# Retention by two chunks at a time: scores in a row, values in a row, K^T V at places of its own

## The chip, the cores and the metric

The kernel runs on one core of a Trainium2 chip. The metric is the device time of one execution in microseconds. "Ratio" is the mean time of one kernel's fast runs over that of the kernel before in the same rounds, so it is not quite the ratio of the medians that stand beside it. "Faster" or "slower" is said of a difference above 2%; smaller ones are called "same", though their intervals may exclude 1.

## The reference

Two stages in fp32: retention (linear attention with a decay by head) and a maxout FFN on its output.

```python
# q, k, v: (8, 8, 576, 64); gamma by head
scores = scale * np.matmul(q, k.transpose(0, 1, 3, 2))
ret = scores * Dmat                      # gamma**(i-j) where i >= j, else 0
attn = np.matmul(ret, v)
x = attn.transpose(0, 2, 1, 3).reshape(4608, 512)
h = np.maximum(np.maximum(x @ w1, x @ w2), x @ w3)     # 512 -> 768
out = h @ w_out                                        # 768 -> 512
```

## The kernel before

The 4608 tokens are cut into 36 chunks of 128 for the retention and into 9 tiles of 512 for the FFN. A sequence of 576 tokens doesn't end with a chunk, so some chunks hold the end of one sequence and the start of the next (`start_of`). Within a chunk, the kernel computes masked scores times values; what lies further back comes from a running state, K^T V summed over chunks.

```python
def load(g, *between):              # 16 small DMAs each for q and kx, then k and v
    for n, src in () if g < BY_PE else (("q", q), ("kx", k)):      # BY_PE: chunks 0-6 go another way
        t = raws[n, g] = raw.tile(..., bufs=3 if n == "q" else 2)
        for blk in range(C // 32):
            for a in range(4):
                nc.sync.dma_start(...)                             # 16 KB each
    ...                                                            # k and v, on nc.sync too
def decay_values(g):                # GpSimd: vd = v * gk
def transposes(g):                  # VectorE: kT from kx, qT from q (g >= BY_PE)
def scores(g):
    for p in range(NP):
        for j in range(2):
            r = slice(D * j, D * (j + 1))                          # 64 rows: two row tiles
            nc.tensor.matmul(s[j][:, p, :], lhsT=kT[r, p, :], rhs=qT[r, p, :], start=True, stop=True)
    ...                                                            # VectorE: mask into st
    r = start_of(g) or 0
    for p in range(NP):                                            # K^T V, in the same visit
        nc.tensor.matmul(kv[:, p, :], lhsT=pair(kr, p)[r:], rhs=pair(vds[g], p)[r:], start=True, stop=True)
    t = states[g + 1] = stp.tile([P, NP, P], FP32, tag="state", name="state")
    ...
        nc.vector.tensor_tensor(t[:], kv[:], states[g][:], op=ALU.add)
        nc.gpsimd.tensor_tensor(t[:], t[:], gs[:], op=ALU.mult)
def values(g):
    ...   # vd x st into o: 64 columns, two column tiles; then state x qT; VectorE: o * gq into xT
```

FFN tile t and the retention of the next four chunks are interleaved by hand. The FFN of a tile is a generator of 12 steps: nine units of up products (Strassen-like, seven products each, from tile 1 on) and three of the down products. Its output stores are issued by SyncE, like all loads; tile 0 also converts the weights from 64-bit floats.

```python
for t in range(N // NT):
    work = ffn(t)
    for g in range((t + 1) * CPT, (t + 2) * CPT):
        for step in (transposes, scores, values):
            if g < NG:
                if step is transposes and g + 1 < NG:
                    load(g + 1)
                if step is scores and g + 1 < NG:
                    decay_values(g + 1)
                if g > CPT or step is not transposes:
                    step(g)
            next(work, None)
```

Of the kernel before, what the change touches and what calls it, by code (L numbers as in the profile page):

```python
# [34 lines left out]
FP32 = mybir.dt.float32  # L35
# [4 lines left out]
ALU = mybir.AluOpType  # L40
PSUM = bass.MemoryType.PSUM

C = 128
NT = 4 * C
# [7 lines left out]
def kernel(  # L52
# [14 lines left out]
    nc = tc.nc  # L67
    P = 128
    B, H, S, D = q.shape
    N, DM = out.shape  # L70
    DF = moe_w1.shape[1]
    NP = H // 2
    NG = B * S // C
    NDC = DM // P
    NF = DF // P
    CPT = NT // C
# [3 lines left out]
    raw = ctx.enter_context(tc.tile_pool(name="raw", bufs=AHEAD + 1))  # L80
    vpool = ctx.enter_context(tc.tile_pool(name="vpool", bufs=3))
    att = ctx.enter_context(tc.tile_pool(name="att", bufs=2))
    stp = ctx.enter_context(tc.tile_pool(name="stp", bufs=2))
    xpool = ctx.enter_context(tc.tile_pool(name="xpool", bufs=2))
    spool = ctx.enter_context(tc.tile_pool(name="spool", bufs=1))
    hpool = ctx.enter_context(tc.tile_pool(name="hpool", bufs=1))
# [5 lines left out]
    ps_r = ctx.enter_context(tc.tile_pool(name="ps_r", bufs=4, space=PSUM))  # L92
# [5 lines left out]
    gq = const.tile([P, NP, C], FP32, name="gq")  # L98
# [17 lines left out]
    def start_of(g):  # L116
        r = -g * C % S
        return r if r < C else None
# [8 lines left out]
    raws, vds, qks, sts, states = {}, {}, {}, {}, {}  # L127

    def spans(g):

        row = 0
        while row < C:
            b, pos = divmod(g * C + row, S)
            n = min(C - row, S - pos)
            yield row, b, pos, n
            row += n

    def load(g, *between):
        rows = (("k", k), ("q", q), ("v", v)) if g < BY_PE else (("k", k), ("v", v))
        for n, src in () if g < BY_PE else (("q", q), ("kx", k)):  # L140

            t = raws[n, g] = raw.tile([P, NP, C // 32, 32], FP32, tag=n, name=n + "raw", bufs=3 if n == "q" else 2)
            for blk in range(C // 32):
                b, pos = divmod(g * C + 32 * blk, S)
                for a in range(4):
                    nc.sync.dma_start(
                        t[32 * a:32 * a + 32, :, blk, :],
                        src[b, a // 2::2, pos:pos + 32, 32 * (a % 2):32 * (a % 2) + 32].rearrange("p j i -> j p i"))
        for n, src in rows:
            if n == "v":  # L150
                for t, what in between:
                    nc.sync.dma_start(t[:], what)
            t = raws[n, g] = raw.tile([C, H, D], FP32, tag=n, name=n + "raw", bufs=4 if n == "k" else 3)
            for row, b, pos, m in spans(g):
                nc.sync.dma_start(t[row:row + m], src[b, :, pos:pos + m, :].rearrange("h p d -> p h d"))  # L155

    def decay_values(g):
        t = vds[g] = vpool.tile([C, H, D], FP32, tag="vd", name="vd")
        nc.gpsimd.tensor_tensor(t[:], raws.pop(("v", g))[:], gk[:].unsqueeze(2).to_broadcast([C, H, D]),  # L159
                                op=ALU.mult)  # L160

    def pair(t, p):
        return t[:, 2 * p:2 * p + 2, :].rearrange("a h d -> a (h d)")

    def transposes(g):
        both = qks[g] = {}
        if g >= BY_PE:
            for n in ("k", "q"):
                t = both[n] = att.tile([P, NP, C], FP32, tag=n + "T", name=n + "T", bufs=2 if n == "k" else 3)
                nc.vector.transpose(t[:].rearrange("a p c -> a (p c)"),  # L170
                                    raws.pop(("kx" if n == "k" else n, g))[:].rearrange("a p b i -> a (p b i)"))
            return
        for n, src in (("k", raws["k", g]), ("q", raws.pop(("q", g)))):
            pt = ps_r.tile([P, NP, C], FP32, tag="r", name=n + "t")
            for p in range(NP):
                nc.tensor.transpose(pt[:, p, :], pair(src, p), ident[:C, :C])
            t = both[n] = att.tile([P, NP, C], FP32, tag=n + "T", name=n + "T", bufs=2 if n == "k" else 3)
            nc.scalar.copy(t[:], pt[:])

    def scores(g):  # L180
        qT, kT = qks[g]["q"], qks[g]["k"]
        s = [ps_r.tile([C, NP, C], FP32, tag="r", name=f"s{j}") for j in range(2)]
        for p in range(NP):
            for j in range(2):
                r = slice(D * j, D * (j + 1))
                nc.tensor.matmul(s[j][:, p, :], lhsT=kT[r, p, :], rhs=qT[r, p, :], start=True, stop=True)  # L186
        st = sts[g] = att.tile([C, 2, NP, C], FP32, tag="st", name="st", bufs=2)
        for j in range(2):
            nc.vector.tensor_tensor(st[:, j], s[j][:], masks[start_of(g)][:].unsqueeze(1).to_broadcast([C, NP, C]),  # L189
                                    op=ALU.mult)  # L190
        kr = raws.pop(("k", g))
        if g + 1 == NG or start_of(g + 1) == 0:
            return
        r = start_of(g) or 0
        kv = ps_r.tile([P, NP, P], FP32, tag="r", name="kv")
# [3 lines that stand above are left out]
        if start_of(g) is not None:  # L199
            nc.vector.tensor_tensor(t[:], kv[:], gs[:], op=ALU.mult)  # L200
        else:
            nc.vector.tensor_tensor(t[:], kv[:], states[g][:], op=ALU.add)
            nc.gpsimd.tensor_tensor(t[:], t[:], gs[:], op=ALU.mult)

    xT, xS = {}, {}

    def values(g):
        old = C if start_of(g) is None else start_of(g)
        t, i = divmod(g, CPT)
        if i == 0:  # L210
            xT[t] = xpool.tile([P, NDC, NT], FP32, tag="xT", name="xT")
        st, vr, qT = sts.pop(g), vds.pop(g), qks.pop(g)["q"]
        o = ps_r.tile([P, NP, C], FP32, tag="r", name="o")
        for p in range(NP):
            for j in range(2):
                nc.tensor.matmul(o[D * j:D * (j + 1), p, :], lhsT=vr[:, 2 * p + j, :], rhs=st[:, j, p, :],  # L216
                                 start=(p == 0), stop=(old == 0 and p == NP - 1), skip_group_check=True)
        if old > 0:
            sd = states.pop(g)
            for p in range(NP):  # L220
                nc.tensor.matmul(o[:, p, :old], lhsT=sd[:, p, :], rhs=qT[:, p, :old],  # L221
                                 start=False, stop=(p == NP - 1), skip_group_check=True)
        nc.vector.tensor_tensor(xT[t][:, :, i * C:(i + 1) * C], o[:], gq[:], op=ALU.mult)  # L223
        if i == CPT - 1 and t > 0:
            x = xT[t]
            a11, a12, a21, a22 = (x[:, 2 * d:2 * d + 2, NH * r:NH * (r + 1)] for r in range(2) for d in range(2))
            s1, s2, s3, s4 = (spool.tile([P, 2, NH], FP32, tag=f"S{n}", name=f"S{n}") for n in (1, 2, 3, 4))
            nc.vector.tensor_tensor(s1[:], a21, a22, op=ALU.add)
            nc.vector.tensor_tensor(s2[:], s1[:], a11, op=ALU.subtract)
            nc.gpsimd.tensor_tensor(s3[:], a11, a21, op=ALU.subtract)  # L230
            nc.gpsimd.tensor_tensor(s4[:], a12, s2[:], op=ALU.subtract)
            xS[t] = {1: a11, 2: a12, 3: s4[:], 4: a22, 5: s1[:], 6: s2[:], 7: s3[:]}
# [200 lines left out]
    def convert(n):  # L433
        for _ in range(n):
            next(converting, None)
# [119 lines left out]
    warm(2)  # L555
    decay_values(1)
    scores(0)
    transposes(1)
    values(0)
    decay_values(2)  # L560
    scores(1)
    transposes(2)
    values(1)
    decay_values(3)
    scores(2)
    transposes(3)
    convert(2)
    values(2)
    convert(2)
    scores(3)  # L570
    decay_values(4)
    convert(2)
    values(3)
    transposes(4)
    convert(4)
    for t in range(N // NT):
        work = ffn(t)
        for g in range((t + 1) * CPT, (t + 2) * CPT):
            for step in (transposes, scores, values):
                if g < NG:  # L580
                    if step is transposes and g + 1 < NG:
                        load(g + 1)
                    if step is scores and g + 1 < NG:
                        decay_values(g + 1)
                    if g > CPT or step is not transposes:
                        step(g)
                next(work, None)


# [49 lines left out]
```

## Time and profile before

| | before |
|---|---|
| median (3 runs) | 830.7 us (830.61 to 830.96) |
| span of the profiled run | 828.2 us |
| TensorE, VectorE busy | 99%, 52% of the span |
| start of tile 1's first product | 130.18 us |
| tiles 1 to 7 (to the start of tile 8) | 622.30 us |
| tile 8 (no retention beside it) | 75.7 us |

The page in 40 equal slices (each digit is the tenths busy, or of full clock), and the head of its chain of work that ended last:

```profile
PE   9999999999999999999999999999999999999998
DVE  3999986455455544544454445444544435533342
PEclk9999999999999999999999999999999999999999
...
PE 86%; DVE 6%; issue 2%; SPq 2%; DMA 2%; ACT 1%; POOL 0%; DVEq 0%
```

TensorE (PE) is full from end to end at full clock, and it makes 86% of the chain. What the time can lose is TensorE work; what it can gain is any wait of TensorE.

### The profile page before, as it was taken

How to read it: one execution, taken by the hardware profiler on the slowest of the kernel's cores; microseconds unless marked ns; L12 is line 12 of the kernel's file. 1: busy time of each engine (PE TensorE's matmuls, PEld its weight loads, DVE VectorE, ACT ScalarE, POOL GpSimd, SP SyncE). 2: the span in 40 equal slices, each digit the busy share in tenths (PEclk: the TensorE clock that was granted, in tenths of full speed). 3: DMA queues.
4: the chain of work that ended last, by engine and by line, in shares of the span. 5: the costliest groups of instructions: out<-in, count | busy, mean ns of one | idle time of the engine just before them, and what ended most of it. 6: DMA issues, size and time to landing. Idle time of an engine off the chain costs nothing.

```text
span 828.2 us, 12659 instructions
## 1 busy us (share of the span) xinstructions
PE 821.8 (99%) x4616; PEld 668.8 (81%) x4616; DVE 434.5 (52%) x805; ACT 173.9 (21%) x401; POOL 192.3 (23%) x182
## 2 busy tenths in 40 slices
PE   9999999999999999999999999999999999999998
PEld 8555547888888888888888888888888888888887
DVE  3999986455455544544454445444544435533342
ACT  3766611111111111110111111111111011111211
POOL 3644665212111120113012111111111202201000
PEclk9999999999999999999999999999999999999999
DMA  9965431343133323332233223332333233201001
GB/s 231 302 169 155 104 70 45 57 79 63 51 55 57 56 79 57 57 57 56 58 73 61 60 52 57 56 58 79 57 57 55 59 75 58 46 13 39 1 1 51
DMA packets 236094, 59.33 MB, mean 72 GB/s; under 512 B 217088, under 2 KB 234496, under 8 KB 236032
## 3 DMA queue, kind: packets, MB, share of 16 engines
q1 hardware_dynamic: 235888, 58.53, 31.6%
q8 instruction: 36, 0.59, 0.3%
q14 instruction: 26, 0.21, 0.1%
q10 hardware_dynamic: 144, 0.00, 0.0%
HBM read 49.03 MB, written 9.44 MB: 71 GB/s over the span
## 4 chain that ended last, share of the span: by engine, by line
PE 86%; DVE 6%; issue 2%; SPq 2%; DMA 2%; ACT 1%; POOL 0%; DVEq 0%
PE x L446 30%; PE z L446 15%; PE dx L319 10%; PE y L446 8%; PE dz L319 5%; PE s L186 4%; PE o L216 4%; PE o L221 3%; PE kv L197 3%; PE dy L319 3%; PE down L495 2%; DVE expo L398 1%; SPq L155 1%; DVE frac L387 1%; DVE mant L393 1%
## 5 line engine op out<-in xcount | busy, mean ns | idle before, releaser
L446 PE MATMUL x<-S,T 128*128 128x256 f32 x576 | 147.9, 379 | 0.0
L159 POOL TENSOR_TENSOR vd<-vraw,gk 128x512 f32<-128x512 f32 x36 | 37.9, 1052 | 361.0 <-DMA vraw<-in_v_dram 342.2
L446 PEld LDWEIGHTS x<-S,T 128*128 128x128 f32 x576 | 109.0, 190 | 15.5 <-ACT u L451 0.3
L446 PE MATMUL x<-xT,w 128*128 128x256 f32 x288 | 74.8, 382 | 0.0
L476 DVE TENSOR_TENSOR tmp<-x,p 128x256 f32<-128x256 f32 x48 | 20.4, 425 | 103.5 <-PE x L446 103.5
L446 PE MATMUL x<-S,w 128*128 128x256 f32 x288 | 74.3, 380 | 0.0
L446 PE MATMUL z<-S,w 128*128 128x256 f32 x288 | 73.9, 379 | 0.0
L446 PE MATMUL y<-xT,w 128*128 128x256 f32 x288 | 73.9, 379 | 0.0
L446 PE MATMUL z<-xT,T 128*128 128x256 f32 x288 | 73.9, 379 | 0.0
L451 ACT COPY p<-x 128x256 f32<-128x256 f32 x72 | 26.8, 372 | 220.2 <-PE x L446 220.2
L189 DVE TENSOR_TENSOR st<-s,causal 128x512 f32<-128x512 f32 x72 | 46.3, 685 | 41.4 <-PE s L186 41.4
L504 PE MATMUL up<-xT,w 128*128 128x512 f32 x144 | 63.5, 594 | 0.2 <-POOL w L404 0.2
L446 PEld LDWEIGHTS z<-S,w 128*128 128x128 f32 x288 | 54.7, 190 | 7.4
L446 PEld LDWEIGHTS y<-xT,w 128*128 128x128 f32 x288 | 54.7, 190 | 7.4
L446 PEld LDWEIGHTS z<-xT,T 128*128 128x128 f32 x288 | 54.5, 189 | 7.7
L446 PEld LDWEIGHTS x<-S,w 128*128 128x128 f32 x288 | 49.3, 189 | 13.3 <-issue 1.3
L223 DVE TENSOR_TENSOR xT<-o,gq 128x512 f32<-128x512 f32 x36 | 24.9, 691 | 66.0 <-PE o L221 59.9
L446 PEld LDWEIGHTS x<-xT,w 128*128 128x128 f32 x288 | 51.5, 190 | 6.6 <-issue 0.8
L297 POOL TENSOR_TENSOR H<-h 128x256 f32<-128x256 f32 x24 | 17.9, 748 | 150.5 <-DVE h L489 150.5
L504 PEld LDWEIGHTS up<-xT,w 128*128 128x128 f32 x144 | 26.7, 190 | 30.7 <-issue 29.9
L465 DVE TENSOR_TENSOR tmp<-y,p 128x256 f32<-128x256 f32 x48 | 20.4, 425 | 52.7 <-PE y L446 52.7
L451 ACT COPY u<-x 128x256 f32<-128x256 f32 x72 | 26.8, 372 | 100.2 <-PE x L446 97.2
(92 smaller groups left out, 1233.6 us busy)
## 6 DMA issues: line engine op xcount, KB each, us to landing
bits<-in_moe_w_dram SPq DMA_DIRECT2D x18, 512.0 KB, 5.0
out_dram<-osb SPq DMA_DIRECT2D x35, 256.0 KB, 2.1
kraw<-in_k_dram SPq DMA_DIRECT2D x32, 256.0 KB, 3.0
vraw<-in_v_dram SPq DMA_DIRECT2D x32, 256.0 KB, 3.4
qraw<-in_q_dram SPq DMA_DIRECT2D x464, 16.0 KB, 1.8
kxraw<-in_k_dram SPq DMA_DIRECT2D x464, 16.0 KB, 1.8
bits<-in_moe_w_out_dram SPq DMA_DIRECT2D x6, 512.0 KB, 4.0
qraw<-in_q_dram SPq DMA_DIRECT2D x6, 256.0 KB, 5.1
```

The source lines that it names most:

```text
L159: nc.gpsimd.tensor_tensor(t[:], raws.pop(("v", g))[:], gk[:].unsqueeze(2).to_broadcast([C, H, D]), op=ALU.mult)
L186: nc.tensor.matmul(s[j][:, p, :], lhsT=kT[r, p, :], rhs=qT[r, p, :], start=True, stop=True)
L189: nc.vector.tensor_tensor(st[:, j], s[j][:], masks[start_of(g)][:].unsqueeze(1).to_broadcast([C, NP, C]), op=ALU.mult)
L197: nc.tensor.matmul(kv[:, p, :], lhsT=pair(kr, p)[r:], rhs=pair(vds[g], p)[r:], start=True, stop=True)
L216: nc.tensor.matmul(o[D * j:D * (j + 1), p, :], lhsT=vr[:, 2 * p + j, :], rhs=st[:, j, p, :], start=(p == 0), stop=(old == 0 and p == NP - ...
L221: nc.tensor.matmul(o[:, p, :old], lhsT=sd[:, p, :], rhs=qT[:, p, :old], start=False, stop=(p == NP - 1), skip_group_check=True)
L223: nc.vector.tensor_tensor(xT[t][:, :, i * C:(i + 1) * C], o[:], gq[:], op=ALU.mult)
L319: nc.tensor.matmul(out[m], lhsT=hS[n](fp)[:, m * P:(m + 1) * P], rhs=late["T"][n][:, fp, :], start=first and fp == 0 and (m == 0 or last a ...
L446: nc.tensor.matmul(out[:], lhsT=w[:, d * P:(d + 1) * P], rhs=xS[t][n][:, d, :], start=first and d == 0, stop=d == 1, skip_group_check=True)
L451: nc.scalar.copy(c[:], src[:])
L465: nc.vector.tensor_tensor(c11, y[:], p1[:], op=ALU.add)
L504: nc.tensor.matmul(ps[:], lhsT=w_sb[i, fb][:, dc * P:(dc + 1) * P], rhs=xT[t][:, dc, :], start=(dc == 0), stop=(dc == NDC - 1))
```

## The change

The intent is fewer changes of TensorE's tiling mode. The scores use TensorE as two tiles of 64 rows, the values as two tiles of 64 columns; a stretch of matmuls in one of the two modes is called a visit here. Two chunks a and b go together: both scores in one visit, both values in one visit, K^T V of each at another step. That needs a third state buffer, and in a tile's first pair b's scores three steps earlier than before (its transposes two). The core of the diff (the splitting of `scores` into `scores` and `state`, and the start-up part, are left out):

```diff
-    stp = ctx.enter_context(tc.tile_pool(name="stp", bufs=2))
+    stp = ctx.enter_context(tc.tile_pool(name="stp", bufs=3))
...
-    def values(g):
+    def values(*chunks):
...   # for all chunks: vd x st; then for all chunks: state x qT, and o * gq
+    def steps(g):
+        todo = [[] for _ in range(3 * CPT)]
+        for n in range(0, CPT, 2):
+            a, b, at = g + n, g + n + 1, 5 * (n // 2)
+            for c, k in ((a, at), (b, at + (g > CPT))):
+                if c + 1 < NG:
+                    todo[k].append(partial(load, c + 1))
+                if c > CPT:
+                    todo[k].append(partial(transposes, c))
+                if c + 1 < NG:
+                    todo[k].append(partial(decay_values, c + 1))
+            todo[at + 1] += [partial(scores, a), partial(scores, b)]
+            todo[at + 2].append(partial(state, a))
+            todo[at + 3].append(partial(state, b))
+            todo[at + 4].append(partial(values, a, b))
+        return todo
+
     for t in range(N // NT):
         work = ffn(t)
-        for g in range((t + 1) * CPT, (t + 2) * CPT):
-            for step in (transposes, scores, values):
...
+        for todo in steps((t + 1) * CPT) if t + 1 < N // NT else [[]] * 3 * CPT:
+            for step in todo:
+                step()
+            next(work, None)
```

More of the change, by code (lines that the diff above doesn't have):

```diff
@@ L190, in scores, with state @@
                                     op=ALU.mult)
+    def state(g):
         kr = raws.pop(("k", g))
@@ L205, with before @@
     xT, xS = {}, {}
-    def values(g):
-        old = C if start_of(g) is None else start_of(g)
-        t, i = divmod(g, CPT)
-        if i == 0:
-            xT[t] = xpool.tile([P, NDC, NT], FP32, tag="xT", name="xT")
-        st, vr, qT = sts.pop(g), vds.pop(g), qks.pop(g)["q"]
-        o = ps_r.tile([P, NP, C], FP32, tag="r", name="o")
-        for p in range(NP):
-            for j in range(2):
-                nc.tensor.matmul(o[D * j:D * (j + 1), p, :], lhsT=vr[:, 2 * p + j, :], rhs=st[:, j, p, :],
-                                 start=(p == 0), stop=(old == 0 and p == NP - 1), skip_group_check=True)
-        if old > 0:
-            sd = states.pop(g)
-            for p in range(NP):
-                nc.tensor.matmul(o[:, p, :old], lhsT=sd[:, p, :], rhs=qT[:, p, :old],
-                                 start=False, stop=(p == NP - 1), skip_group_check=True)
-        nc.vector.tensor_tensor(xT[t][:, :, i * C:(i + 1) * C], o[:], gq[:], op=ALU.mult)
+    def values(*chunks):
+        def before(g):
+            return C if start_of(g) is None else start_of(g)
+        o = {g: ps_r.tile([P, NP, C], FP32, tag="r", name="o") for g in chunks}
+        for g in chunks:
+            st, vr = sts.pop(g), vds.pop(g)
+            for p in range(NP):
+                for j in range(2):
+                    nc.tensor.matmul(o[g][D * j:D * (j + 1), p, :], lhsT=vr[:, 2 * p + j, :], rhs=st[:, j, p, :],
+                                     start=(p == 0), stop=(before(g) == 0 and p == NP - 1), skip_group_check=True)
+        for g in chunks:
+            t, i = divmod(g, CPT)
+            qT, old = qks.pop(g)["q"], before(g)
+            if old > 0:
+                sd = states.pop(g)
+                for p in range(NP):
+                    nc.tensor.matmul(o[g][:, p, :old], lhsT=sd[:, p, :], rhs=qT[:, p, :old],
+                                     start=False, stop=(p == NP - 1), skip_group_check=True)
+            if i == 0:
+                xT[t] = xpool.tile([P, NDC, NT], FP32, tag="xT", name="xT")
+            nc.vector.tensor_tensor(xT[t][:, :, i * C:(i + 1) * C], o[g][:], gq[:], op=ALU.mult)
         if i == CPT - 1 and t > 0:
@@ L557 @@
     scores(0)
+    state(0)
     transposes(1)
@@ L561 @@
     scores(1)
+    state(1)
     transposes(2)
@@ L565 @@
     scores(2)
+    state(2)
     transposes(3)
@@ L570 @@
     scores(3)
+    state(3)
     decay_values(4)
@@ L575 @@
     convert(4)
+    def steps(g):
[14 more added lines that the diff above has]
+        return todo
     for t in range(N // NT):
         work = ffn(t)
-        for g in range((t + 1) * CPT, (t + 2) * CPT):
-            for step in (transposes, scores, values):
-                if g < NG:
-                    if step is transposes and g + 1 < NG:
-                        load(g + 1)
-                    if step is scores and g + 1 < NG:
-                        decay_values(g + 1)
-                    if g > CPT or step is not transposes:
-                        step(g)
-                next(work, None)
+        for todo in steps((t + 1) * CPT) if t + 1 < N // NT else [[]] * 3 * CPT:
+            for step in todo:
+                step()
+            next(work, None)
 _INS = ['q', 'k', 'v', 'moe_w1', 'moe_w2', 'moe_w3', 'moe_w_out']
```

## The prediction

> **What bounds the kernel now.** I read the page's busy table first, then the windows by stage, then the merged timeline of one steady stage on TensorE, SyncE, VectorE and GpSimd, and last the waits. Tile t of the FFN (512 tokens) runs while the retention of the next four chunks is worked in between; a tile has 12 steps, nine "units" (7 Strassen products each) and three of the down projection.
>
> ```profile
> PE 821.8 (99%) x4616; PEld 668.8 (81%) x4616; DVE 434.5 (52%) x805; ACT 173.9 (21%) x401; POOL 192.3 (23%) x182
> ...
> 27.70:130.00 102.30, 101.59 (x401) 51.93 (x401) 97.45 (x142) 52.79 (x81) 63.18 (x47) 1.00 0.52 144
> 218.20:308.00 89.80, 89.80 (x530) 76.91 (x529) 43.35 (x83) 13.75 (x38) 15.84 (x15) 1.00 0.30 60
> ```
>
> The window lines give length, then PE, PEld, DVE, ACT, POOL busy, clock, DMA share and GB/s. From tile 1 on TensorE is the bound without a gap, at full clock; in tile 0 (27.7 to 130) VectorE is nearly as full (97.5 of 102.3), since it converts the weights. So a saving must be TensorE time, and any stall of TensorE is paid in full.
>
> Where TensorE loses time inside the retention shows in the start times (start, length, line, what):
>
> ```profile
> 222.48 1.03 PE L446 MATMUL z<-xT,T 128*128 128x256 f32 x4
> 223.34 1.08 PE L446 MATMUL x<-S,w 128*128 128x256 f32 x4
> 224.35 1.16 PE L186 MATMUL s<-qT,kT 64*128 64x128 f32 x16
> 225.44 1.16 PE L197 MATMUL kv<-vd,kraw 128*128 128x128 f32 x8
> 226.44 1.03 PE L446 MATMUL x<-xT,w 128*128 128x256 f32 x4
> ...
> 231.62 1.03 PE L446 MATMUL x<-S,w 128*128 128x256 f32 x4
> 232.58 1.09 PE L216 MATMUL o<-st,vd 128*64 128x128 f32 x16
> 233.60 1.16 PE L221 MATMUL o<-qT,state 128*128 128x128 f32 x8
> 234.59 1.03 PE L446 MATMUL x<-xT,w 128*128 128x256 f32 x4
> ```
>
> An ordinary product takes 0.86 us from start to start (222.48 to 223.34); the one before the scores takes 1.01. The scores use 64 rows (two row tiles), the values 64 columns (two column tiles), all else the full array.
>
> The second thing that matters is how the data of the next chunk come in:
>
> ```profile
> 218.16 1.03 PE L446 MATMUL x<-xT,w 128*128 128x256 f32 x4
> 218.36 0.65 ACT L369 COPY osb<-dx 128x256 f32<-128x256 f32 x2 [9.24 <-PE dx L319]
> 219.46 7.61 SPq L146 DMA_DIRECT2D qraw<-in_q_dram  x16
> 227.10 8.49 SPq L146 DMA_DIRECT2D kxraw<-in_k_dram  x16
> 235.69 1.28 SPq L155 DMA_DIRECT2D kraw<-in_k_dram  x2
> 237.07 1.27 SPq L155 DMA_DIRECT2D vraw<-in_v_dram  x2
> ...
> 242.44 0.70 DVE L170 STREAM_TRANSPOSE kT<-kxraw 128x512 f32<-128x512 f32 x1
> 243.06 0.66 DVE L170 STREAM_TRANSPOSE qT<-qraw 128x512 f32<-128x512 f32 x1
> 246.78 1.16 PE L186 MATMUL s<-qT,kT 64*128 64x128 f32 x16
> ```
>
> A load of one chunk keeps SyncE busy for 17 to 19 us: 32 small DMAs of q and k at 0.47 us of issue each, plus k and v. This load (chunk b, the tile's second) starts at 219.46, only after the last output store of the tile before, which waits for ScalarE's copy at 218.36. Its last transposable k lands at 236.85, its v at 240.77 (landing times in the trace). Before, VectorE wants it at 242.44, a little later, so nobody pays. The waits confirm that SyncE's queue stops at stores and that GpSimd's value decay always waits for v:
>
> ```profile
> SPq L333 <- DVE osb L338: 183.4, 23, 58.9
> POOL vd L159 <- DMA vraw<-in_v_dram: 342.2, 31, 25.8
> ```
>
> **What the Trainium skill says.** "TensorEngine Tiling (Array Packing)", Key Properties: changing the tiling mode drains the array, changing only the tile does not. The trace agrees: single starts in it are 309 ns apart from the last ordinary matmul to the first score (216 otherwise), then 207 from first to second pair (112 otherwise), 201 out, and 320 for the first ordinary one after (216). "PSUM — Partial Sum Buffer", Engine vs sequencer instructions: VectorE, ScalarE and GpSimd take their queues strictly in order. "TensorE: Matmul & The Clock Gate", Part 3, The mechanism: matmuls are strictly in order too. The trace shows no overtaking. Same page, Part 1: after an idle window of some 3.4 us the clock halves, and comes back after some 3.4 us of work. The trace starts so (128-column matmuls 213 ns apart instead of 112) and never falls back, as no long gap exists.
>
> **The change part by part.** It drops no arithmetic. *Fewer switches.* A visit of the scores costs 1.720 us from the last matmul before to the second after, against 0.216 + 8 x 0.112 + 0.216 = 1.328 of streaming: 0.39 of switching. A visit of the values: 1.547 against 0.216 + 8 x 0.109 + 0.112 = 1.20: 0.35. Two chunks in a row save one visit of each, 0.74 us, and the main loop has 32 chunks, 16 pairs: 11.8 us, 1.4%. Moving K^T V elsewhere saves nothing itself: it only carried the exit of the scores, which the next product now carries. *A third state buffer* costs nothing.
>
> *The moved order.* With 12 steps for four chunks, chunk b's load is still issued at step 0 but its transposes are now at step 1, before step 1's scores, instead of step 3. Relative to step 0's start (218.16): the load starts at 1.3, kx lands at 18.7, transposes end near 20.5 (two of 0.7, 0.63 apart, and 0.4 of waits). TensorE has unit 0 (28 x 0.216 = 6.05) and a's scores (1.1) and stands at 7.2: a stall of 13.3 us. The same buffers let the second pair's loads (b at step 6) run ahead, kx landing near 55, so there TensorE waits only for VectorE's tail of the unit and two transposes: some 1.9.
>
> *GpSimd in order.* The decay for the chunk after b is put at step 1 and waits for v landing at about 40; the state multiply of a stands behind it (to 42.7), and b's state addition on VectorE waits for that, with the FFN's evictions behind. Following unit 3 with 0.42 us evictions, product 3 starts at 45.4 instead of 40.7: 4.6 us more where both states are ordinary (tiles 4 to 7), about 1 us in tiles 2 and 3, none in tile 1.
>
> Summing a tile: step 0 6.05; step 1 ends 27.7; step 2 34.6; step 3 46.2 (or 41.6 to 42.7); step 4 with 3.9 of retention 56.2; step 5 62.2; step 6 72.3; 7 79.2; 8 86.2; 9 (3.9 + 5.2) 95.3; 10 100.4; 11 (7.8) 108.2. Against 89.8 now that is +18.4 with the state stall, +15.2 or +14.7 without: 4 x 18.4 + 2 x 15.2 + 14.7 = 119 us, the saving of the switches already in it.
>
> *Tile 0* puts b's transposes in the same step as its load. Step 0: TensorE waits for chunk 5 (k and q landed 34.7 and 35.7) instead of starting at 27.7: +8. Step 5: VectorE meets the transposes of chunk 7 when SyncE has just begun its load: some 18 us, with the weight conversions behind, and GpSimd then waits for chunk 8's v another 17. TensorE has units in hand for part of it. I put tile 0 at +28 in all.
>
> *The clock.* Each stall of 13 us is long enough to halve it; 3.4 to 6.8 us at half speed loses 1.7 to 3.4, say 2.6: 7 x 2.6 and a little in tile 0 = 20 (an estimate from the page of the clock gate).
>
> Sum: 830.7 + 119 + 28 + 20 = 998. I take 985, as the chain of late starts also gives other queues time to catch up.
>
> **The rivals.** *The switches alone count:* 830.7 - 11.8 = 819, still within 2%. For it: the bound is TensorE and the switches are real. Against: it needs b's load before step 1, and the store in front of it on SyncE forbids that. *Only the SyncE stall counts*, and GpSimd, tile 0 and clock are hidden: 7 x (13.3 - 1.5) = 83, less 1.5 in tile 0, so 912. Against: the queues are in order, so they are not free. *VectorE becomes the bound* through four mask multiplies (0.69 each) in one step: 2.8 us in a step of 8 where it is 48% busy; this hides and changes nothing.
>
> **Range and chances.** 912 with everything hidden but the sure stall, 998 with all: 985, eight in ten in 935 to 1030. Faster by 2% is out of reach even without stalls (1.4%): 0.01. Within 2% needs my reading of the load's order to be wrong: 0.03. Slower: 0.96.
>
> **What would show it.** Right: TensorE gaps of about 13 us between the two score groups of a tile's first pair, released by VectorE's transposes, and these by kxraw DMAs; VectorE idle "<- DMA kxraw"; matmuls at double spacing after each gap; half as many 309 ns entries; GpSimd's state multiply waiting for vraw. Wrong: SyncE issuing b's q and k before the last stores, or a TensorE that stays at 99% busy.

## The result, and the profile after

The changed kernel takes **975.13 us** (median of 4 runs, 973.34 to 976.04) against 830.65 of the kernel before in the same rounds (4 runs): ratio 1.174 (1.172 to 1.176), slower. The profiled run has a span of 974.3 us.

The same parts of its page, with the busy line:

```profile
PE 842.6 (86%) x4616; PEld 691.2 (71%) x4616; DVE 443.1 (45%) x805; ACT 174.3 (18%) x401; POOL 187.5 (19%) x182
...
PE   9697599599949995999778995999599996999998
...
PEclk9799799799979998899979997999889997999999
...
PE 65%; SPq 20%; DVE 6%; DMA 4%; issue 4%; POOL 1%; ACT 1%; DVEq 0%; POOLq 0%; ACTq 0%
```

The number of matmuls is the same, 4616. Holes come in TensorE's row once a tile, each with a dip in the clock at or just after it, and SyncE's queue (SPq) now makes 20% of the chain. So the time went into waits for loads, not into work.

The windows of tiles 1 to 7, before and then after (columns as in the prediction):

```profile
130.18:752.48 622.30, 622.30 (x3641) 531.84 (x3640) 296.95 (x582) 96.17 (x265) 112.17 (x112) 1.00 0.29 58
```

```profile
160.85:898.66 737.81, 637.02 (x3642) 549.94 (x3641) 303.56 (x586) 96.28 (x265) 113.31 (x111) 0.93 0.24 49
```

The span grew by 146.1 us: tile 0 by 30.7, tiles 1 to 7 by 115.5, tile 8 not at all. The first pair of a steady tile, tile 1, in the timeline after (start, length, engine, line, what; in brackets the idle time before it and what ended it):

```profile
161.71 0.33 SPq L509 DMA_DIRECT2D out_dram<-osb  x1
162.13 7.53 SPq L146 DMA_DIRECT2D qraw<-in_q_dram  x16
166.99 1.16 PE L186 MATMUL s<-qT,kT 64*128 64x128 f32 x16
169.71 7.54 SPq L146 DMA_DIRECT2D kxraw<-in_k_dram  x16
178.84 0.71 DVE L170 STREAM_TRANSPOSE kT<-kxraw 128x512 f32<-128x512 f32 x1 [11.85 <-DMA kxraw<-in_k_dram]
179.47 0.67 DVE L170 STREAM_TRANSPOSE qT<-qraw 128x512 f32<-128x512 f32 x1
180.29 2.08 PE L186 MATMUL s<-qT,kT 64*128 64x128 f32 x16 [12.13 <-DVE qT L170]
```

Read from the top: SyncE issues the last store of the tile before, then b's load. TensorE does a's scores at 166.99, while half of that load is not even issued. VectorE waits 11.85 us for the last kx, transposes, and TensorE's next scores come at 180.29, 12.40 us after the start of the last matmul before. They take 2.08 us instead of 1.16: the clock is down.

What TensorE, VectorE and GpSimd waited for over the whole run (total, times, longest):

```profile
POOL vd L159 <- DMA vraw<-in_v_dram: 425.3, 27, 32.8
PE s L186 <- DVE qT L170: 103.6, 15, 13.7
DVE kT L170 <- DMA kxraw<-in_k_dram: 100.5, 8, 13.8
PE x L456 <- DVE h L486: 4.5, 3, 2.7
```

The first line's total is large, but GpSimd has little to do, so by itself it says nothing; the second is TensorE's time, and the third shows where it comes from. The saving is there too, as the values of two chunks in one visit:

```profile
202.34 1.97 PE L221 MATMUL o<-st,vd 128*64 128x128 f32 x32
204.24 1.16 PE L229 MATMUL o<-qT,state 128*128 128x128 f32 x8
```

To split the 115.5 us, I sorted the gaps between the starts of neighbouring matmuls in tiles 1 to 7 into waits (over 1.2 us), excess at half clock, and the rest above streaming (mode changes above all):

| tiles 1 to 7, us | before | after |
|---|---|---|
| streaming | 600.1 | 600.1 |
| waits | 0 | 103.9 |
| excess at half clock | 0 | 22.0 |
| mode changes and the rest | 22.2 | 11.8 |

The waits are seven gaps in the first pairs (12.40, 12.76, 12.56, 12.19, 12.44, 13.96, 12.28 from start to start: 88.6), seven in the second pairs (1.92 and six of 1.60: 11.5) and two ahead of the third product of a unit (3.08 and 1.89), less the ordinary interval of each.

Tile 0 shows three waits of its own: for chunk 5's load, for chunk 7's transposes, and for GpSimd, which makes the weights and had stood at a load of v:

```profile
35.26 1.09 PE L176 MATMUL kt<-ident,kraw 128*128 128x128 f32 x4 [7.37 <-DMA kraw<-in_k_dram]
97.66 2.08 PE L186 MATMUL s<-qT,kT 64*128 64x128 f32 x16 [7.26 <-DVE qT L170]
119.34 2.08 PE L514 MATMUL up<-xT,w 128*128 128x512 f32 x2 [10.46 <-POOL w L414]
```

The clock's half-speed stretches there cost another 6.8 us.

### The profile page after: what moved, and what is told of

It reads as the page before. It is cut to its first block, busy times and chain, and to the rows that moved or that the text cites. A ratio compares the mean times of both kernels' runs of the same rounds, so it can differ in the third digit from the quotient of the medians.

```text
span 974.3 us, 12654 instructions
## 1 busy us (share of the span) xinstructions
PE 842.6 (86%) x4616; PEld 691.2 (71%) x4616; DVE 443.1 (45%) x805; ACT 174.3 (18%) x401; POOL 187.5 (19%) x182
## 4 chain that ended last, share of the span: by engine, by line
PE 65%; SPq 20%; DVE 6%; DMA 4%; issue 4%; POOL 1%; ACT 1%; DVEq 0%; POOLq 0%; ACTq 0%
PE x L456 20%; SPq L146 18%; PE z L456 9%; PE dx L329 9%; PE y L456 5%; PE dz L329 4%; PE up L514 3%; PE o L221 3%; PE o L229 3%; PE s L186 2%; PE kv L200 2%; PE dy L329 2%; PE down L505 2%; DMA kxraw<-in_k_dram 1%; DMA vraw<-in_v_dram 1%
## 5 line engine op out<-in xcount | busy, mean ns | idle before, releaser
L186 PE MATMUL s<-qT,kT 64*128 64x128 f32 x576 | 48.9, 317 | 103.6 <-DVE qT L170 103.6
L186 PEld LDWEIGHTS s<-qT,kT 64*128 64x128 f32 x576 | 41.8, 218 | 112.7 <-issue 111.6
L456 PE MATMUL x<-xT,w 128*128 128x256 f32 x288 | 83.0, 414 | 0.0
L456 PE MATMUL y<-xT,w 128*128 128x256 f32 x288 | 78.4, 397 | 0.0
L514 PE MATMUL up<-xT,w 128*128 128x512 f32 x144 | 68.3, 630 | 10.5 <-POOL w L414 10.5
L170 DVE STREAM_TRANSPOSE kT<-kxraw 128x512 f32<-128x512 f32 x29 | 20.4, 705 | 100.5 <-DMA kxraw<-in_k_dram 100.5
L456 PEld LDWEIGHTS y<-xT,w 128*128 128x128 f32 x288 | 58.6, 204 | 9.2
L456 PEld LDWEIGHTS x<-xT,w 128*128 128x128 f32 x288 | 54.9, 204 | 9.3 <-issue 2.0
```

Source lines behind the costliest of these rows:

```text
L170: nc.vector.transpose(t[:].rearrange("a p c -> a (p c)"), raws.pop(("kx" if n == "k" else n, g))[:].rearrange("a p b i -> a (p b i)"))
L456: nc.tensor.matmul(out[:], lhsT=w[:, d * P:(d + 1) * P], rhs=xS[t][n][:, d, :], start=first and d == 0, stop=d == 1, skip_group_check=True)
L514: nc.tensor.matmul(ps[:], lhsT=w_sb[i, fb][:, dc * P:(dc + 1) * P], rhs=xT[t][:, dc, :], start=(dc == 0), stop=(dc == NDC - 1))
```

## The experiments

My theory: pairing does save its mode changes, but b's load is issued after the last stores of the tile before, whose wait holds SyncE's queue; its transposes now come two steps too early for that. The rivals: TensorE's own new order costs (a mode change more dearly than it saves), GpSimd's order or the clock alone sets the time, or tile 0 does most of it. All runs gave correct results.

| run | median us | before, same rounds | ratio (95%) | tiles 1–7, us |
|---|---|---|---|---|
| the change | 975.13 | 830.65 | 1.174 (1.172–1.176) | 737.81 |
| e1 stores on ScalarE | 876.07 | 830.45 | 1.055 (1.053–1.057) | 636.80 |
| e9 one load ahead of the stores | 864.57 | 830.72 | 1.041 (1.039–1.042) | 626.87 |
| e2 before, b's transposes early | 914.60 | 830.45 | 1.101 (1.099–1.104) | 707.25 |
| e6 tile 0 in the old order | 945.33 | 830.45 | 1.138 (1.137–1.140) | 737.91 |
| e5 matmuls in the gap | 985.15 | 830.45 | 1.186 (1.183–1.189) | 748.81 |
| e10 decay later | 969.08 | 830.13 | 1.167 (1.166–1.169) | 731.76 |
| e11 both of these | 962.86 | 830.13 | 1.162 (1.158–1.166) | 724.24 |
| e3 before, values in pairs | 829.65 | 830.75 | 0.9985 (0.997–1.000) | 617.75 |
| e4 before, scores cut in two | 842.57 | 830.75 | 1.014 (1.012–1.015) | 630.69 |
| e7 pairs with loads ahead | 824.47 | 830.75 | 0.992 (0.991–0.994) | 616.24 |
| e8 the same, a seam mended | 823.31 | 830.72 | 0.990 (0.988–0.992) | 613.59 |

### Is it the store in front of the load? (e1, e9)

e1 keeps the new order and issues all output stores from ScalarE:

```diff
-            nc.sync.dma_start(block.rearrange(...), osb[:, blocks])
+            nc.scalar.dma_start(block.rearrange(...), osb[:, blocks])
...   # and the same in down(), for tile 0
```

> The changed kernel with one edit: the output stores are issued from ScalarE's queue, so they no longer stand in front of chunk b's load on SyncE. If the 13 us stalls come from that order on SyncE, the seven gaps between the first pair's two score groups vanish with their clock losses; what stays is tile 0 (+30.7 us as measured) and 1.6 us of VectorE's tail per second pair, against 1.5 us of saved switches: about 862 us, 845 to 880. If the stalls come from the pairing itself (PSUM banks, four mask multiplies in one step), the time stays near 975.

Measured: 876.07 us, 99 us below the changed kernel. The seven gaps of 12 us are gone; of the waits of tiles 2 to 7 only the 1.60 us in each second pair are left. That is inside the range, some 14 us above its middle; 9 of these are tile 1, which took 99.6 us where tile 2 took 90.5. The timeline shows why:

```profile
156.93 0.58 ACT L508 COPY osb<-down 128x512 f32<-128x512 f32 x1 [4.57 <-PE down L505]
...
163.98 7.65 SPq L146 DMA_DIRECT2D kxraw<-in_k_dram  x16
...
168.31 0.37 ACTq L509 DMA_DIRECT2D out_dram<-osb  x1
...
168.78 0.58 ACT L508 COPY osb<-down 128x512 f32<-128x512 f32 x1 [11.27 <-DMA kxraw<-in_k_dram]
...
172.54 2.07 PE L456 MATMUL x<-S,T 128*128 128x256 f32 x4 [8.77 <-ACT p L461]
```

ScalarE also evicts the FFN's products, in order. The copy of 156.93 is done at 157.51, but its store is issued only at 168.31, and the next copy, and the eviction of a product of tile 1 (p), stand behind it. As releaser of ScalarE the profile names a kx load, and the trace's semaphores show why. All DMAs of this program, from both issuers, take turns on eight semaphores, and before each one its issuer waits until the last DMA on the same semaphore has landed; for this store that was a kx load that landed at 168.23. That load was chunk 10's, not b's: SyncE, no longer held by stores, had run ahead and stood from 149.6 until VectorE's transposes (done at 163.95) freed a buffer. So a store from ScalarE is not free of SyncE's loads here. Moving a wait to another queue moved its victim.

e9 leaves the stores on SyncE and moves only the one load in question to step 7 of the tile before, ahead of the stores:

```diff
-                if c + 1 < NG:
+                if c + 1 < NG and (k > 0 or g == CPT):
                     todo[k].append(partial(load, c + 1))
...
+        if g + 5 < NG:
+            todo[7].append(partial(load, g + 5))
```

> The changed kernel with one load moved: in tiles 1 to 7 the load of the first pair's chunk b is asked for at step 7 of the tile before, ahead of the output stores; all steps of TensorE, VectorE and GpSimd stay. If the order on SyncE is the cause, the seven gaps of 12 to 14 us and the halved clock after them go, and 1.6 us per second pair and tile 0's 30.7 us stay: 862, 857 to 868. If the gaps came from the early transposes or the pairing as such, it stays at 975.

Measured: 864.57 us, within the range: 110.6 us of the 144.5 that the change costs go away by where one load stands. The timeline of tile 1's first pair, now:

```profile
166.98 1.16 PE L186 MATMUL s<-qT,kT 64*128 64x128 f32 x16
...
168.91 1.16 PE L186 MATMUL s<-qT,kT 64*128 64x128 f32 x16 [0.76 <-DVE qT L170]
```

1.9 us between the two scores instead of 13.3, both at full clock. In tiles 1 to 7 there is no half clock any more, and the only waits over 1.2 us are the seven of 1.60. What is left above the kernel before is tile 0 (it ends at 160.48) and these waits.

### Is it the early transposes rather than the pairing? (e2)

The old order, with nothing paired; only b's transposes go to step 1 in tiles 1 to 7.

```diff
+                    if t > 0 and g % CPT == 0 and step is scores:
+                        transposes(g + 1)
-                    if g > CPT or step is not transposes:
+                    if (g > CPT or step is not transposes) and not (t > 0 and g % CPT == 1 and step is transposes):
                         step(g)
```

> The kernel before with one edit: in tiles 1 to 7 the second chunk's transposes are put at step 1, ahead of the first chunk's mask multiplies, nothing is paired. If the early transposes alone cause the loss, VectorE stands at kxraw as in the changed kernel; TensorE goes on through 5.2 us of the unit and stops at product 3, about 8 to 10 us per tile plus 2 us of halved clock: 895 to 920. If pairing is what costs, it stays at 831.

Measured: 914.60 us, as expected. Every tile has one gap of 8.9 to 11.8 us (67.1 us above streaming), and the half clock takes 20.1. Here TensorE doesn't wait for scores but for VectorE's eviction of a product, since VectorE stands at the transposes with the FFN's evictions behind it. The pairing is not needed for the loss: early transposes of a late load are enough.

### How much is tile 0? (e6)

```diff
+    def one_by_one():                # load g+1, transposes g | decay g+1, scores g, state g | values g
...
-        for todo in steps((t + 1) * CPT) if t + 1 < N // NT else [[]] * 3 * CPT:
+        for todo in one_by_one() if t == 0 else steps((t + 1) * CPT) if t + 1 < N // NT else [[]] * 3 * CPT:
```

> The changed kernel, but tile 0 works its four chunks one by one in the old order. Tile 0 then ends at 130 us instead of 161 and nothing else moves: 975 - 31 = 944, 938 to 950. If the loss of tile 0 is made up later anyway, the time stays above 955.

Measured: 945.33 us, 29.8 below the changed kernel; tile 1 starts at 131.25. So tile 0 is its own loss of some 30 us, and it adds to the rest.

### What does the clock cost? (e5, e10, e11)

e5 gives TensorE 48 throw-away matmuls of the identity in each 12-us gap of tiles 1 to 7. They write the banks that the scores then overwrite.

```diff
+        if g > 2 * CPT and g % CPT == 1:
+            for n in range(48):
+                nc.tensor.matmul(s[n % 2][:, 0, :], lhsT=ident[:], rhs=ident[:], start=True, stop=True)
```

> The changed kernel with 48 identity matmuls (96 passes of 0.112 us, 10.8 us) put before the second score group of each tile's first pair, into banks that the scores then overwrite; they fill a gap of 12.2 to 14 us in which TensorE stood. If the halved clock costs what I read (22 us of excess at half clock in tiles 1 to 7, most of it after these gaps), the time falls by 10 to 20 us, to 955 to 965, with the clock at full speed over the seven gaps. If the clock costs nothing, the time stays at 975 or grows.

Measured: 985.15 us, **a miss**: 10 us slower, not 10 to 20 faster. The excess at half clock fell from 22.0 to 15.8 us in tiles 1 to 7, but other terms grew. The wait ahead of a unit's third product, seen twice after the change, now stands in all of tiles 4 to 7 (5.25, 3.13, 3.97, 4.36 us from start to start). The longest, in the timeline:

```profile
516.77 2.08 PE L459 MATMUL x<-S,w 128*128 128x256 f32 x4 [4.87 <-DVE h L489]
```

This is the state wait of the prediction: GpSimd's decay waits for v, the state multiply stands behind it, b's state addition on VectorE behind that, and the FFN's evictions behind all. When TensorE isn't slowed before, it meets that wait earlier and waits longer. After the matmuls 1.8 to 3.1 us of pause were left in each gap (17.7 in all), so they took 75.3 us (672 passes of 0.112, as the trace shows each of the 336 matmuls as two) in place of 70.9 of waiting (88.6 − 17.7). So the run doesn't measure the clock alone.

e10 moves the decay of the chunk after b behind b's state (without the extra matmuls):

```diff
-                if c + 1 < NG:
+                if c + 1 < NG and (c == a or g == CPT):
                     todo[k].append(partial(decay_values, c + 1))
...
+            if b + 1 < NG and g > CPT:
+                todo[at + 3].append(partial(decay_values, b + 1))
```

> The changed kernel, in tiles 1 to 7 with GpSimd's decay of the chunk after b put behind b's state step instead of ahead of a's, so that the state multiply no longer waits for a v that lands late. The changed kernel waited for it in tiles 4 and 5 alone (3.1 and 1.9 us before product 3): 975 - 4.5 = 970.6, 968 to 973. If those two waits have another cause, 975.

Measured: 969.08 us, 6 below the changed kernel, and no wait ahead of a third product is left: that wait is GpSimd's order, and after the change it costs some 5 us. e11 has both edits:

> The kernel with identity matmuls in the gap, with the same move of the decay. With the clock kept up it showed the state wait in four tiles (5.3, 3.1, 4.0, 4.4 us) where the changed kernel showed two. If the halved clock had only hidden that wait, the move now frees it: 985 less 15.8 of waiting and some 5 of half clock after it, 965 to 971, below the move without the matmuls or level with it. If the identity matmuls cost by themselves, it stays above 975.

Measured: 962.86 us, 6.2 below e10 and 22.3 below e5, a little under the range that I gave. The windows of tiles 1 to 7 of e5 and of e11:

```profile
160.36:909.17 748.81, 707.86 (x4313) 620.64 (x4312) 303.22 (x585) 96.17 (x265) 112.14 (x111) 0.98 0.24 49
```

```profile
159.76:884.00 724.24, 699.30 (x4313) 615.24 (x4312) 300.02 (x586) 96.28 (x265) 111.80 (x111) 0.99 0.25 50
```

With the same matmuls, e11 is 24.6 us shorter. Against e10 its half-clock excess is 13.1 us less (7.7 for 20.8), and 6 of these reach the end; the extra matmuls give the others back. So the clock does cost time, but the state wait and the clock hide one another: moving the decay brings 6 us without the matmuls and 22 with them; the matmuls cost 10 us with the state wait and bring 6 without it. The last 6 is the weakest of these: e11's four runs scatter from 961.35 to 968.86, and the ratios' intervals of e10 and e11 just touch.

### Does a mode change cost what was read? (e3, e4)

e3 takes only the paired values into the kernel before (three state buffers, scores as they were):

```diff
-                    if g > CPT or step is not transposes:
+                    if step is values:
+                        if g % 2:
+                            values(g - 1, g)
+                    elif g > CPT or step is not transposes:
                         step(g)
```

> The kernel before with one part of the change alone: the values of two chunks in a row, everything else in the old order and at the old steps. If a visit of the column tiles costs 0.35 us, 16 visits fewer make 830.7 - 5.5 = 825.2 (823.5 to 827). If the gain of fewer switches is only apparent, it stays at 830.7.

Measured: 829.65 us, **a miss in the total**. Tiles 1 to 7 gave 4.55 us as expected (617.75 for 622.30; 14 visits fewer, 0.325 each). But tile 1 started at 134.15 instead of 130.18: at the end of tile 0 TensorE waited for the last of the weights,

```profile
PE down L502 <- POOL w_out L411: 3.3, 2, 3.0
```

and the clock went down for 3.4 us after it. The conversion that ended the long wait was done at 108.91 where it was done at 107.52 in the kernel before; GpSimd had stood in front of it at a v, until 99.68 where it was 98.25. Why that v lands later when the values are paired I did not test.

e4 makes the opposite: each scores visit of the kernel before is cut in two by its K^T V, one visit of row tiles more for most chunks.

```diff
+        some(range(0, NP // 2))
+        ...                                  # K^T V, as before
+        some(range(NP // 2, NP))
```

> The kernel before with the suspected cost doubled: each visit of the scores is cut in two halves with K^T V between them (28 of the 32 chunks of the main loop, and four at the start). If a visit costs 0.39 us of switching, that adds 28 x 0.39 = 11 us or a little more: 841 to 844. If switching costs nothing, it stays at 831.

Measured: 842.57 us, 11.8 above the kernel before. The trace has 21 visits more in tiles 1 to 7 (42 mode changes), and these tiles took 8.39 us more: 0.40 each, for the 0.39 that was read from the start times. (The rest comes before tile 1, which starts 4.64 us later in the profiled run, with seven visits more.) The rival that a mode change is free, or far dearer, falls.

### Can the intent be had? (e7, e8)

e7 pairs in tiles 1 to 7, with tile 0 in the old order, both chunks' loads issued up to two chunks ahead and before the stores, both transposes at the step before the scores, and the decays behind the states (lines joined; the code of tile 0 is left out, it asks for one load more at its end):

```diff
+        at(0, transposes, g);  at(1 if first else 0, transposes, g + 1)
+        if first: at(1, decay_values, g + 1)
+        at(0, load, g + 2);    at(2, load, g + 3)
+        at(5, transposes, g + 2); at(5, transposes, g + 3); at(5, decay_values, g + 3)
+        at(5, load, g + 4);    at(7, load, g + 5)
+        for n, k in ((0, 0), (2, 5)):        # a, b = g + n, g + n + 1
+            at(k + 1, scores, a); at(k + 1, scores, b)
+            at(k + 2, state, a);  at(k + 3, state, b); at(k + 3, decay_values, b + 1)
+            at(k + 4, values, a, b)
+        at(10, decay_values, g + 5)
```

> Pairs as in the change for tiles 1 to 7, but every chunk is loaded two chunks ahead, so that both chunks of the next tile's first pair are asked for before the output stores; both transposes of a pair stand a step ahead of its scores; the decay of a later chunk stands behind the state multiplies; tile 0 as before. If the switches are the gain and the waits the whole loss, 14 pairs x 0.74 = 10.4 us less than before: 820, 818.5 to 824. If SyncE's 70 us of loads a tile now delay the stores or the loads, 824 to 840.

Measured: 824.47 us, just above the range I gave for success and at the lower end of the one for loads in the way. Of the waits over 1.2 us in tiles 1 to 7 one is left, 2.88 us in tile 1, where VectorE stood at chunk 11's kx. e8 puts that tile's second pair one step later (steps 6 and 11 for 5 and 10).

> The kernel of loads two chunks ahead with tile 1's second pair one step later, since there VectorE stood 3.4 us at the k of chunk 11, whose load had come late behind tile 0's stores, and TensorE 2.7 us after it. If that was the rest of the way to the 10.4 us that 14 pairs should give, the time falls from 824.5 to 821 (820 to 822.5). If the missing 4 us are elsewhere, it stays at 824.

Measured: 823.31 us (821.82 to 824.31), ratio 0.990 (0.988 to 0.992). It beats both kernels, though "same" by the 2% measure, and it lies 0.8 us above the range. Tiles 1 to 7 have no wait over 1.2 us and take 613.59 us, 8.7 less than before. At the end of tile 0, two waits for the last weights (1.66 and 1.36 us from start to start) and 3.4 us of half clock put tile 1's start at 133.34 in the profiled run, 3.2 later than before. It is the same seam as in e3, and it stays open.

## Why the prediction was right or wrong

The time (975 for 985) and the direction were right, and most of its mechanism was seen in the trace after and tested. By its own terms:

- **Switches, −10.4 in tiles 1 to 7 (14 pairs at 0.74).** The sorted gaps give −10.4, but eight mode changes lie in waits or at half clock and are counted there. Undisturbed, in e8, it is −8.7. The step "Moving K^T V elsewhere saves nothing itself: it only carried the exit of the scores" missed that it can cost: of three chunks that start a sequence 64 rows in (13, 22, 31), K^T V uses 64 rows. Before, it followed the scores in the same mode without a change (111 ns from start to start). At a place of its own it is a visit of its own: 31 visits are left in tiles 1 to 7 where there were 56, not 28. At 0.39 each that is 1.2 of the missing 1.7 us.
- **The stall of the first pair, 13.3 a tile, 93.1 for seven.** Measured 88.6. e1 and e9 show that it is the load's place behind the stores, e2 that early transposes alone bring it.
- **The second pair, 1.9 a tile, 13.3.** Measured 11.5.
- **The state wait, "4.6 us more where both states are ordinary (tiles 4 to 7), about 1 us in tiles 2 and 3": 20 in all.** This is the term that was mis-sized most: 3.08 us in tile 4 and 1.89 in tile 5 from start to start, nothing in the others. e10 confirms the mechanism and a size of 6 us in the time. The prediction summed each tile with TensorE at full clock between the stall and this wait. In truth TensorE runs part of that stretch slowed, and, as I read it, mostly comes late enough not to wait. In e5, with less of the half clock, it waits in all four tiles.
- **The clock, 20.** Measured 22.0 in tiles 1 to 7 alone, where 18 was meant, and 6.8 in tile 0, where it was meant as "a little". As excess it was under-sized. As an addition to the state wait it was wrong, as these hide one another (e5, e10, e11).
- **Tile 0, 28.** Measured 30.7, and 29.8 by e6, of which 6.8 is half clock. The wait of 8 us for chunk 5 was 7.37; that for chunk 7 was 7.26 where 18 lay behind work in part; and GpSimd's standing at v showed in 10.46 us of waiting for weights.
- **The sum.** The steps gave 998 and 985 was chosen "as the chain of late starts also gives other queues time to catch up". The surplus of 23 us was some 15 of state wait and 6 of the two stalls, less 4 of clock; the rest lies in the rounding of its sums (the terms for tiles 1 to 7 make 116, its steps 119) and between spans and medians. The reason given for the discount was a guess that no run tests, so that 985 came nearer than 998 is partly luck.

The rival "only the SyncE stall counts", 912, is refuted by e6 and by the half-clock excess; "VectorE becomes the bound" by e8, where the pairs run in tiles 1 to 7 without a wait over 1.2 us; "the switches alone count", 819, describes e8 and not the change.

## What to carry to other kernels

Before moving an instruction earlier in a hand-made order, find when its data can be there at the earliest, and for a load that is when the queue issuing it comes past everything in front of it: here one store in each tile, waiting at the head of SyncE's queue, cost over 100 us in all in a change worth 9. Two losses that follow each other in one chain (here a slower clock, then a wait) need not add up: test them singly and together before adding them. A saving of mode changes could be read from start times to about a tenth of a microsecond a pair (0.74 read, 0.62 in e8 with the three K^T V visits against it), and was then still partly lost at a seam elsewhere.

## What the Trainium skill lacked or had wrong

- "TensorEngine Tiling (Array Packing)", Key Properties, says that changing the tiling mode drains TensorE and gives no cost. Here a visit of row tiles cost about 0.39 us by the start times (0.40 in e4: 8.39 us for 21 added visits), and one of column tiles 0.325 (e3: 4.55 us for 14). It speaks of row tiling at 64 rows as something to use; that a single matmul over 64 rows is in that mode by itself it doesn't say: K^T V over 64 rows after the scores ran on without a change (0.111 us), and among matmuls of 128 rows it cost two changes (0.309 in, 0.320 for the first ordinary one after, for 0.216).
- "TensorE: Matmul & The Clock Gate", table "Why this matters for your kernels", advises no TensorE gap over about 3 us. In the changed kernel and in e10 the clock was halved for 3.41 us after a pause of 1.92 us (218.31 and 218.93), so 3 us is not a safe limit. But the length alone doesn't decide it: the six pauses of 1.60 and one of 1.89 in the changed kernel, 2.88 in e7 and 3.11 in e5 were not followed by it. Around each gap of 12 to 14 us in the changed kernel the records show 13.65 us at half clock; TensorE works in the last 3.7 to 5.7 of them, somewhat more than the "some 3.4 us" of Part 1 for the way back.
- "DMA: Bandwidth & Descriptors", section "Issuing engines are not separate DMA queues", says that issuing from several engines saves only the sequencer's issue time, usually small beside the DMA. Here 32 DMAs of 16 KB took 0.47 us of issue each, 15 us for a chunk, and a waiting store in front held them back further: with stores issued from ScalarE (e1) the kernel was 99 us faster than with all on SyncE. The page doesn't tell that a wait ahead of a DMA blocks the later ones of the same issuer (nor does "Perfetto Trace Analysis", section "DMA Optimizations", where it suggests one issuing engine for inputs and another for outputs), nor that issuing from an engine with work of its own can stall that work: in e1 a store of ScalarE stood 10.8 us (157.51 to 168.31) behind a semaphore shared with SyncE's loads, and TensorE lost 8.77 us to it.
